# Which gaps the writes and sums of weight parts stand in: attention and gated MLP on one core

## The chip, the core and the metric

The kernel runs on one core of one Trainium2 chip. TensorE (PE) multiplies, VectorE (DVE) and ScalarE (ACT) work element by element, SyncE (SP) issues most of the DMAs (transfers between the chip's memory, called DRAM here, and the on-chip buffers). The metric is the device time of one launch in microseconds (us), the median of three runs.

## The reference

Two parts follow each other. In a chunked attention, each chunk of 32 queries sees 8 memory tokens, 16 tokens to the left, its own 32 and 8 to the right. Then the 3072 resulting tokens of width 512 go through an RMS norm and a gated MLP with 1536 features:

```python
for c in range(nc):                       # 4 batches x 8 heads, 24 chunks
    scores = scale * np.matmul(q_c, k_full.transpose(0, 1, 3, 2))
    scores = scores - np.max(scores, axis=-1, keepdims=True)
    a = np.exp(scores)
    a = a / (np.sum(a, axis=-1, keepdims=True) + 1e-09)
    out[:, :, c_start:c_end] = np.matmul(a, v_full)
...
x = np.ascontiguousarray(attn_out.transpose(0, 2, 1, 3)).reshape(B * S, H * D)
...
rms = np.sqrt(np.mean(x * x, axis=-1, keepdims=True) + 1e-06)
xn = x / rms * rms_g
g = xn @ w_gate
silu = g * (1.0 / (1.0 + np.exp(-g)))
val = xn @ w_val
return (silu * val @ w_out).astype(np.float32)
```

Every product of the MLP keeps float32 accuracy by splitting both factors into a high and a low part and adding three products: high by high, low by high, high by low.

## The kernel before

**Stages.** The tokens are cut in blocks of 384. An order written out by hand (`ORDER`) does the attention of the first two blocks, splits the first weights and starts the MLP. Then three segments follow: the rest of block 0 (features 5 to 11), block 2 (features 0 to 11) and block 3 (all twelve, 10 and 11 first). At the end `whole(2)` and `whole(3)` each take two blocks together, by a scheme with seven products in place of eight. It multiplies by sums and differences of weight quarters. These, and the plain weight parts, are read back from scratch in DRAM (the tiles `kept`: `kg` for the gate weight, `kv` for the value weight, `ko` for the output weight), which the segments write.

**A segment.** For the n-th feature group of 128 it issues 12 matmuls of the gate product (`pg`, L469), then calls `visit(2n)`, 12 of the value product (`pv`), `visit(2n+1)`, 9 of the output product of the feature before (`po`, L519), `visit(2n+1.5)`, and then the elementwise part of its own feature: a tanh (L483), the gate (L487, reading the bank `pg`), the product with `pv` (L490), its high part `hh` (L178) and low part `hl` (L499). The number that `visit` is called with is the gap. At the end of block 0 and block 2 the last feature takes another path: the gate product is copied to `rg` (L478), and after L487 and L490 the next block's x is split (L750) and the last `hh` is made (L753).

**What a gap does**, in this order:
- `dumps(k)` writes plain weight parts from their buffers to scratch: six DMAs on SyncE (L767), two of 256 KB, two of 128 KB and two of 256 KB. There are twelve such items. They are pinned behind the last DMA issued on SyncE so far.
- `keep(n)` spends a budget of n elements a partition on the weight sums, from the table `KEEP`. An item of sums has two additions 512 wide (high plus low part, L803, at 512 each of the budget), four additions or subtractions 256 wide (L806), four casts on ScalarE into the buffer `kh` (L810), two subtractions 512 wide (L815), and two writes of 512 KB on SyncE (L817 from `kh`, L819 from the sums `ks` or `qp1`). It costs 3072 of budget. There is a single `kh`, and it shares a buffer with `rg`: the casts of the next item wait until the write from it has ended.
- The letters in the table `VISITS` step the attention of a later pair of heads: "p" transposes the probabilities of the pair before (L279) and copies them out of their banks (L178 on ScalarE, L181 on VectorE); "s" makes the scores of the next pair (L216), takes maxima (L227), subtracts (L239), takes exponentials (L244), and, when these scores have been made, loads the queries (L163) and keys (L165) of the pair after into the same buffers; "o" (half a gap later) makes the value product of the pair (banks `oe` and `oo`, L310), evacuates it (L321, into `xT`), squares it (L324), and loads the next values (L170); "n" does a piece of the RMS norm.

**What sets the order.** TensorE's instructions stay in program order. The other engines' pieces are placed by a scheduler, within what `issue_after` pins, and each engine runs its queue in order: an instruction that waits holds all behind it. A DMA on SyncE that waits for its buffer does the same. Before the change, gaps 0 to 11 of block 0 call `dumps` once each.

Of the kernel before, what the change touches and what calls it, by code (L numbers as in the profile page):

```python
# [8 lines left out]
F32 = mybir.dt.float32  # L9
# [14 lines left out]
DM, FF = 512, 1536  # L24
P = 128
# [21 lines left out]
PAIRS = tuple((f, f + 1) for f in range(0, FF // P, 2))  # L47
NR = 30

KEEP = {0: {2: 1024, 3: 1024},  # L50
# [3 lines left out]

CHAIN = (("g", 1, "a", 1), ("g", 2, "c", 1), ("v", 1, "a", 1), ("g", 6, "a", 0), ("v", 2, "c", 1), ("g", 7, "a", 0),
         ("v", 6, "a", 0), ("g", 5, "e", 1), ("g", 4, "a", 0), ("v", 7, "a", 0), ("g", 3, "e", 0), ("v", 5, "e", 1),
# [30 lines left out]
def tile_kernel(ctx: ExitStack, tc: tile.TileContext, q, k, v, w_gate, w_val, w_out, rms_g, out):  # L87
# [11 lines left out]
    dram = ctx.enter_context(tc.tile_pool(name="dram", bufs=1, space=bass.MemoryType.DRAM))  # L99
# [174 lines left out]
    def stage_p(u, tag=None):  # L274
        d = st[u]
        t = psum_m(tag, f"pT{u}") if tag else psum_a(f"pT{u}")
        pe = d["p"].rearrange("p j k -> p (j k)")
        for i in range(NT):
            on_pe(nc.tensor.transpose(out=t[:, i * P:(i + 1) * P], in_=pe[:, i * P:(i + 1) * P], identity=ident))  # L279
        d["t"] = t  # L280
# [183 lines left out]
    def moe_in(n, f, xs, kts=range(NKT), ps=None):  # L464
        if ps is None:
            ps = psum_m(n, f"p{n}")
        for kt in kts:
            for i, (a, c) in enumerate(PASS):
                on_pe(nc.tensor.matmul(ps[:, 0:HT], lhsT=weight(a, n, f, kt), rhs=xs[c][:, kt],  # L469
                                 start=kt == 0 and i == 0, stop=kt == NKT - 1 and i == 2))  # L470
        return ps[:, 0:HT]
# [37 lines left out]
    def moe_h(g, vv, blk):  # L509
        t = moe_t(g, vv, blk)  # L510
        return moe_hl(t, moe_hh(t))

    def psm_o(i):
        return psum_m(f"o{i}", f"po{i}")

    def moe_out(f, h, po, first=0, end=NF - 1):
        for i in range(NT):
            for n, (a, c) in enumerate(PASS):
                on_pe(nc.tensor.matmul(po[i], lhsT=h[a][:, i * P:(i + 1) * P], rhs=weight(c, "o", f),  # L519
                                 start=f == first and n == 0, stop=f == end and n == 2))  # L520
# [4 lines left out]
    def store(blk, po):  # L525
        for i in range(NT):
            o = obuf(f"ob{i}")
            nc.scalar.activation(o, po[i], AF.Copy, scale=0.5 if blk > 1 else sh[blk][:, i:i + 1])
            nc.scalar.dma_start(out=out[blk * HT + i * P:blk * HT + (i + 1) * P], in_=o)
# [23 lines left out]
    def last_of(eng):  # L553
        return next(i for i in reversed(nc.cur_bb.bb.instructions) if i.engine == eng.engine)
# [136 lines left out]
    def tok_o(n):  # L691
# [10 lines left out]
        P=lambda n: stage_p(n, "o0" if n < NG else None),  # L702
# [58 lines left out]
    kept = {}  # L761

    def dump(f, w, cols, to):
        k, i, n = fgroup[f]
        for part in range(2):
            c = wt[part, w, k].bitcast(F32)[:, i * DM:(i + 1) * DM]
            nc.sync.dma_start(out=to[:, :, part], in_=c[:, cols].rearrange("p (k f) -> p k f", k=to.shape[1]))  # L767

    items, sums = [(p, w) for p in (5, 0, 1, 2, 3, 4) for w in "gv"], {}

    def dumps(k):
        p, w = items[k]
        fa, fb = PAIRS[p]
        kept[w, p] = t = dram.tile([P, 7, 2, DM // 2], F32, name=f"k{w}{p}")
        with tc.issue_after(last_of(nc.sync)):
            dump(fa, w, slice(0, DM), t[:, 0:2])
            dump(fb, w, slice(DM // 2, DM), t[:, 2:3])
            f = fa if w == "g" else fb
            kept["o", f] = t = dram.tile([P, 2, DM], F32, name=f"ko{f}")
            dump(f, "o", slice(0, DM), t.unsqueeze(1))  # L780

    def keep_steps():

        late_part = iter(())
        for k in range(len(items) + 1):
            now = keep_item(k) if k < len(items) else iter(())
            for _ in range(2):
                if k < len(items):
                    yield next(now)
            yield from late_part  # L790
            if k < len(items):
                for _ in range(4):
                    yield next(now)
            late_part = now

    def keep_item(k):
        p, w = items[k]
        fa, fb = PAIRS[p]
        s = (late["tmp"] if k % 2 else p1.tile([P, 2 * DM], F32, name="ks", tag="wy")).rearrange("p (k f) -> p k f", k=4)
        for i, f in enumerate((fb, fa)):  # L800
            c, n, _ = fgroup[f]
            h, l = (wt[part, w, c][:, n * DM:(n + 1) * DM].bitcast(F32).rearrange("p (k f) -> p k f", k=2) for part in range(2))
            nc.vector.tensor_tensor(out=s[:, 2 * i:2 * i + 2], in0=h, in1=l, op=ALU.add)  # L803
            yield DM
        for o, a, b, op in ((1, 0, 1, ALU.add), (0, 2, 0, ALU.subtract), (2, 1, 2, ALU.subtract), (3, 3, 2, ALU.subtract)):
            nc.vector.tensor_tensor(out=s[:, o], in0=s[:, a], in1=s[:, b], op=op)  # L806
            if o == 3:
                h = p1.tile([P, 3 * HT], F32R, name="kh", tag="rg")[:, 0:2 * DM].rearrange("p (k f) -> p k f", k=4)
                for i in range(4):
                    nc.scalar.copy(h[:, i], s[:, i])  # L810
            yield DM // 2
        l, t = s.bitcast(F32R), kept[w, p]
        for i in range(2):
            c = slice(2 * i, 2 * i + 2)
            nc.vector.tensor_tensor(out=l[:, c], in0=s[:, c], in1=h[:, c].bitcast(F32), op=ALU.subtract)  # L815
            if i:
                nc.sync.dma_start(out=t[:, 3:7, 0], in_=h.bitcast(F32))  # L817
                with tc.issue_after(last_of(nc.sync)):
                    nc.sync.dma_start(out=t[:, 3:7, 1], in_=s)  # L819
            yield DM  # L820

    keeping = keep_steps()

    def keep(n):
        with tc.issue_after(last_of(nc.vector)), tc.issue_after(last_of(nc.scalar)):
            while n > 0:
                n -= next(keeping, DM)
# [150 lines left out]
    for blk, fs in segments:  # L978
        po = [psm_o(i) for i in range(NT)] if blk else sp["po", 0]
        edge = dict(first=fs[0] if blk else 0, end=fs[-1])  # L980

        def visit(gap):
            if blk == 0 and gap in range(12):
                dumps((gap + 2) % 12)
            keep(KEEP[blk].get(gap, 0))
            for c in VISITS[blk].get(gap, ""):
                if next(todo) != c:
                    raise AssertionError(gap)
        for n, f in enumerate(fs):
            g = moe_in("g", f, xs)  # L990
            visit(2 * n)
            out_ = lambda f=fs[n - 1], h=prev: moe_out(f, h, po, **edge)
            if n == 0:
                out_ = lambda: None
                if blk == 0:

                    moe_out(NF - 1, prev, po1)
                    with tc.high_priority():
                        store(1, po1)
            vv = moe_in("v", f, xs)  # L1000
            visit(2 * n + 1)
            if n < len(fs) - 1:
                out_()
                visit(2 * n + 1.5)
                prev = moe_h(g, vv, blk)
                if blk == 3 and n == 2:
                    late_cm[1].__exit__(None, None, None)
                if blk == 3 and n == 7:
                    w0_cm.__exit__(None, None, None)
                    xpool = ctx.enter_context(tc.tile_pool(name="xs", bufs=1, reuse_waits="tile"))  # L1010
                    sup["ring"] = ctx.enter_context(tc.tile_pool(name="ring", bufs=NR, reuse_waits="tile"))
                    for m in (1, 2, 3, 6):
                        sup["xpool", m] = xpool
                    load(NR)
                    x_first(4)
                if blk == 3 and n == 9:
                    x_second(4)
            elif blk < 3:
                with tc.high_priority():
                    t = moe_t(g, vv, blk)  # L1020
                xs = split_x(late_x["x"], t, out_, lambda h: moe_out(fs[-1], h, po, **edge))
            else:
                with tc.high_priority():
                    h = moe_h(g, vv, blk)
                out_()
        if blk == 0:
            behind.close()
        if blk < 3:
            store(blk, po)
# [84 lines left out]
```

## Time and profile before

| what | value |
|---|---|
| time, median of 3 runs | 698.16 us (697.62 to 699.15) |
| the profiled execution | 696.32 us |
| its span, first to last instruction | 694.5 us |
| TensorE busy / VectorE / ScalarE | 667.8 / 471.5 / 305.0 us |
| moved by DMA | 140.19 MB, 202 GB/s over the span |

The profile is of one execution. Busy time of an engine is what its instructions take; a busy share near 100% says that the engine sets the pace there. In rows of the timeline the first number is the start in us from the span's start, the second the duration, then engine, line, operation, result and operands; brackets at the end give idle time of that engine just before it and what ended that. In rows of the view by windows stand the window, its length, busy time and instructions of PE, PEld (weight loads of TensorE), DVE, ACT and POOL, then the clock that TensorE was granted (1.00 is full speed), the share of time in which the DMA engines were busy, and GB/s. Rows of DMAs give the count, KB each, and the median us from issue to landing.

### The profile page before, as it was taken

Reading aid. Unit: us, or ns where it says so; the run is one execution under the profiler, and the core shown is the slowest. Engines: PE = TensorE matmul, PEld = TensorE weight load, DVE = VectorE, ACT = ScalarE, POOL = GpSimd, SP = SyncE. Lnnn points to the kernel's source line nnn. Section 1 sums busy time; section 2 is a strip of 40 time slices with the busy share of each in tenths; the row PEclk is TensorE's granted clock in tenths of the full one; section 3 lists DMA queues with packets and bytes.
Section 4 is the critical chain, followed back from the end, with each engine's and each line's share of the span. In section 5 each row is a group of like instructions: output and inputs, shape, how many; then the busy total and the mean of one; then the engine's idle time right before and its main releaser. Section 6 shows DMA issues by size and latency. Waiting matters only on the chain.

```text
span 694.5 us, 15083 instructions
## 1 busy us (share of the span) xinstructions
PE 667.8 (96%) x6134; PEld 609.5 (88%) x6134; DVE 471.5 (68%) x937; ACT 305.0 (44%) x566; POOL 4.7 (1%) x12
## 2 busy tenths in 40 slices
PE   7799999999699999999999999999999999999997
PEld 6698899998598898889999899998988899999885
DVE  6788999867478898867858766569639254555221
ACT  4787987832235444344234444343334343332112
POOL 0010000000000000000000000000000000000000
PEclk9999999999999999999999999999999999999999
DMA  9653643449996746337139688887643598885002
GB/s 326 248 179 126 238 156 106 148 153 371 322 375 233 232 152 203 116 99 254 58 108 356 234 255 282 266 294 237 192 143 123 177 301 252 251 254 160 0 1 91
DMA packets 79701, 140.19 MB, mean 202 GB/s; under 512 B 7440, under 2 KB 33040, under 8 KB 79632
## 3 DMA queue, kind: packets, MB, share of 16 engines
q1 hardware_dynamic: 77760, 136.08, 58.6%
q10 hardware_dynamic: 1872, 3.15, 1.2%
q8 instruction: 48, 0.79, 0.5%
q14 instruction: 21, 0.17, 0.1%
HBM read 104.60 MB, written 34.60 MB: 200 GB/s over the span
## 4 chain that ended last, share of the span: by engine, by line
PE 75%; DVE 11%; DMA 5%; ACT 5%; issue 2%; SPq 1%; ACTq 0%; DVEq 0%
PE po L957 14%; PE pv L469 10%; PE pg L469 10%; PE po L519 10%; PE mga L928 7%; PE mva L928 7%; PE mve L928 3%; PE mge L928 3%; PE oe L310 2%; PE mvc L928 2%; PE s L216 2%; PE pT L279 2%; DMA r<-kg 1%; PE mgc L928 1%; DVE t L487 1%
## 5 line engine op out<-in xcount | busy, mean ns | idle before, releaser
L957 PE MATMUL po<-r,hhs 128*128 128x512 f32 x288 | 90.7, 396 | 0.0
L469 PE MATMUL pv<-xh,wh_v 128*128 128x384 f32 x192 | 65.8, 343 | 2.2 <-DVE t L490 1.3
L469 PE MATMUL pg<-xh,wh_g 128*128 128x384 f32 x192 | 66.7, 347 | 0.4 <-DVE t L487 0.4
L469 PE MATMUL pg<-xl,wh_g 128*128 128x384 f32 x192 | 65.4, 341 | 0.5 <-DVE xl L654 0.5
L469 PE MATMUL pv<-xh,wl_v 128*128 128x384 f32 x192 | 65.1, 339 | 0.5 <-DVE wl_v L440 0.5
L469 PE MATMUL pg<-xh,wl_g 128*128 128x384 f32 x192 | 65.5, 341 | 0.0
L469 PE MATMUL pv<-xl,wh_v 128*128 128x384 f32 x192 | 65.1, 339 | 0.0
L957 PEld LDWEIGHTS po<-r,hhs 128*128 128x128 f32 x288 | 53.9, 188 | 12.4
L519 PE MATMUL po<-wh_o,hh 128*128 128x512 f32 x144 | 58.3, 405 | 0.8 <-ACT hh L753 0.4
L928 PE MATMUL mga<-x,r 128*128 128x384 f32 x288 | 58.3, 337 | 0.2 <-ACT spare L900 0.2
L928 PE MATMUL mva<-x,r 128*128 128x384 f32 x288 | 58.1, 337 | 0.1
L519 PE MATMUL po<-wh_o,hl 128*128 128x512 f32 x144 | 57.4, 398 | 0.0
L519 PE MATMUL po<-wl_o,hh 128*128 128x512 f32 x144 | 57.2, 397 | 0.0
L957 PE MATMUL po<-r,hls 128*128 128x512 f32 x144 | 56.8, 395 | 0.0
L939 DVE TENSOR_TENSOR hls<-h,hhs 128x768 fp32r<-128x768 f32 x24 | 22.9, 955 | 42.1 <-ACT hhs L938 42.1
L928 PEld LDWEIGHTS mga<-x,r 128*128 128x128 f32 x288 | 50.5, 188 | 1.0 <-ACT spare L900 0.5
L928 PEld LDWEIGHTS mva<-x,r 128*128 128x128 f32 x288 | 50.5, 188 | 0.5 <-DVE h L911 0.4
L178 ACT CAST hh<-t 128x384 fp32r<-128x384 f32 x46 | 23.7, 514 | 47.4 <-PE po L519 35.7
L938 ACT CAST hhs<-h 128x768 fp32r<-128x768 f32 x24 | 20.0, 835 | 54.4 <-PE po L957 50.5
L469 PEld LDWEIGHTS pv<-xh,wh_v 128*128 128x128 f32 x192 | 36.3, 189 | 4.0 <-DVE t L490 1.6
L469 PEld LDWEIGHTS pg<-xh,wh_g 128*128 128x128 f32 x192 | 36.3, 189 | 2.8 <-DVE t L487 0.9
L469 PEld LDWEIGHTS pg<-xl,wh_g 128*128 128x128 f32 x192 | 36.4, 189 | 2.1 <-DVE xl L654 0.7
(162 smaller groups left out, 1424.6 us busy)
## 6 DMA issues: line engine op xcount, KB each, us to landing
r<-kg SPq DMA_DIRECT2D x84, 256.0 KB, 3.3
r<-kv SPq DMA_DIRECT2D x84, 256.0 KB, 3.3
r<-ko SPq DMA_DIRECT2D x48, 256.0 KB, 3.1
kv<-in_v_dram SPq DMA_DIRECT2D x24, 384.0 KB, 5.3
kv<-in_k_dram SPq DMA_DIRECT2D x24, 312.0 KB, 4.7
ws<-in_moe_w_gate_dram SPq DMA_DIRECT2D x4, 1024.0 KB, 4.9
ws<-in_moe_w_val_dram SPq DMA_DIRECT2D x4, 1024.0 KB, 4.9
ws<-in_moe_w_out_dram SPq DMA_DIRECT2D x4, 1024.0 KB, 5.0
```

Of the source, the lines that this page charges most:

```text
L178: return nc.scalar.copy(out, in_)
L216: on_pe(nc.tensor.matmul(d["s"][a:a + CH, o:o + KC], lhsT=d["q"][r, c * CH:c * CH + CH], rhs=d["k"][r, c // 2, 40 * cp:40 * cp + KC], star ...
L279: on_pe(nc.tensor.transpose(out=t[:, i * P:(i + 1) * P], in_=pe[:, i * P:(i + 1) * P], identity=ident))
L310: on_pe(nc.tensor.matmul(o2[cp][64 * hh:64 * hh + 64, o:o + CH], lhsT=st[u]["v"][r, j, hh], rhs=pt[r, j, hh ^ u % 2], start=True, stop=True))
L469: on_pe(nc.tensor.matmul(ps[:, 0:HT], lhsT=weight(a, n, f, kt), rhs=xs[c][:, kt], start=kt == 0 and i == 0, stop=kt == NKT - 1 and i == 2))
L487: nc.vector.scalar_tensor_tensor(out=t, in0=t, scalar=1.0, in1=g, op0=ALU.add, op1=ALU.mult)
L519: on_pe(nc.tensor.matmul(po[i], lhsT=h[a][:, i * P:(i + 1) * P], rhs=weight(c, "o", f), start=f == first and n == 0, stop=f == end and n = ...
L928: on_pe(nc.tensor.matmul(bank[w, b], lhsT=r[:, a, kt], rhs=x[:, c, kt], start=bool(first) and kt == 0 and i == 0, stop=kt == 1 and i == 2, ...
L938: nc.scalar.copy(hh, sup["h", f])
L939: nc.vector.tensor_tensor(out=hl, in0=sup["h", f], in1=hh.bitcast(F32), op=ALU.subtract)
L957: on_pe(nc.tensor.matmul(po[i], lhsT=cur[a][:, i * P:(i + 1) * P], rhs=r[c], start=f == n == 0, stop=f == NF - 1 and n == 2))
```

## The change

Two tables change. `DUMPS` is new and says how many of the twelve items each gap writes, in the order in which they come: in block 0 one in gaps 1 and 2, none in gaps 3 to 7, then two, one, two, one, one and one in gaps 8 to 13, and the last two in gaps 0 and 1 of block 2. `KEEP` gets a gap 12 in block 0 (1536), gives up half of gaps 4 and 16 and all of gap 18 in block 2, and moves budget in block 3 from gap 4 to gaps 2 and 10. The scratch tiles are allocated up front. A line of the changed kernel has a number higher by 2 in most of the code, by 5 from the sums on.

```diff
-KEEP = {0: {2: 1024, 3: 1024},
-        2: {0: 512, 1: 2048, 2: 2048, 3: 2048, 4: 2048, 6: 512, 7: 1024,
-            8: 2048, 9: 2048, 10: 2048, 11: 2048, 12: 2048, 13: 2048, 14: 2048, 15: 2048, 16: 2048, 18: 512},
-        3: {2: 1024, 3: 2048, 4: 2048, 6: 512, 10: 1024}}
+KEEP = {0: {2: 1024, 3: 1024, 12: 1536},
+        2: {0: 512, 1: 2048, 2: 2048, 3: 2048, 4: 1024, 6: 512, 7: 1024, 8: 2048, 9: 2048, 10: 2048, 11: 2048, 12: 2048, 13: 2048,
+            14: 2048, 15: 2048, 16: 1024},
+        3: {2: 1536, 3: 2048, 4: 1024, 6: 512, 10: 3072}}
+
+DUMPS = {0: {1: 1, 2: 1, 8: 2, 9: 1, 10: 2, 11: 1, 12: 1, 13: 1}, 2: {0: 1, 1: 1}, 3: {}}
...
-    items, sums = [(p, w) for p in (5, 0, 1, 2, 3, 4) for w in "gv"], {}
+    items = [(p, w) for p in (5, 0, 1, 2, 3, 4) for w in "gv"]
+    for p, w in items:
+        kept[w, p] = dram.tile([P, 7, 2, DM // 2], F32, name=f"k{w}{p}")
 
     def dumps(k):
+        k = (k + 2) % len(items)
         p, w = items[k]
         fa, fb = PAIRS[p]
-        kept[w, p] = t = dram.tile([P, 7, 2, DM // 2], F32, name=f"k{w}{p}")
+        t = kept[w, p]
...
-    keeping = keep_steps()
+    keeping, dumping = keep_steps(), iter(range(len(items)))
...
         def visit(gap):
-            if blk == 0 and gap in range(12):
-                dumps((gap + 2) % 12)
+            for _ in range(DUMPS[blk].get(gap, 0)):
+                dumps(next(dumping))
             keep(KEEP[blk].get(gap, 0))
```

TensorE's list of instructions is the same before and after. On the other engines the order moves at these places.

**SyncE in block 0.** The queue of before at the loads of the visits at gap 5 (first four rows) and gap 7 (the rows behind the marks); `q0` and `qp1` are queries, `kv0` and `kv1` keys and values; of the 24 dump DMAs between them the first and the last three stand here:

```order
L163 DMA q0_1702<-in_q_dram 128x384
L165 DMA kv0_1704<-in_k_dram 128x624
L163 DMA qp1_1726<-in_q_dram 128x384
L165 DMA kv1_1727<-in_k_dram 128x624
L767 DMA kg1_1889<-wh_g1_90 128x2x256
...
L767 DMA kv2_1982<-wl_v3_1079 128x256
L767 DMA ko5_1987<-wh_o3_1080 128x512
L767 DMA ko5_1987<-wl_o3_1081 128x512
L163 DMA q0_1702<-in_q_dram 128x384
L165 DMA kv0_1704<-in_k_dram 128x624
L163 DMA qp1_1726<-in_q_dram 128x384
L165 DMA kv1_1727<-in_k_dram 128x624
```

And in the changed kernel, from the same loads on; between the two rows of dumps stand 52 more, nine items in all, and behind them come the first item's write from `kh` (L822) and from `ks`, then the last item's six:

```order
L165 DMA q0_1702<-in_q_dram 128x384
L167 DMA kv0_1704<-in_k_dram 128x624
L165 DMA qp1_1726<-in_q_dram 128x384
L167 DMA kv1_1727<-in_k_dram 128x624
L172 DMA kv0_1704<-in_v_dram 128x768
L172 DMA kv1_1727<-in_v_dram 128x768
L769 DMA kg1_1735<-wh_g1_90 128x2x256
...
L769 DMA ko10_2586<-wl_o6_1483 128x512
L822 DMA kg5_1731<-kh_1919 128x4x256
L824 DMA kg5_1731<-ks_1899 128x4x256
L769 DMA kv5_1732<-wh_v6_1480 128x2x256
```

The dumps have moved from between the loads to behind the last loads of block 0; the write from `kh`, which stood behind twelve items before too, is now nearer to block 2, since nine items are issued only after gap 7.

**VectorE at the end of block 0**, before (`hl` of the feature before, the copy of the last gate product, the gate, the value, then the split of x):

```order
L499 TENSOR_TENSOR hl_2503<-t_2497,hh_2501 128x384
L478 TENSOR_TENSOR rg_154<-pg_2505,rg_154 128x384
L487 SCALAR_TENSOR_TENSOR t_2532<-t_2532,rg_154 128x384
L490 TENSOR_TENSOR t_2532<-t_2532,pv_2518 128x384
L750 TENSOR_TENSOR xl_2537<-xT_1990,xh_2536 128x384
L754 TENSOR_TENSOR hl_2550<-t_2532,hh_2549 128x384
```

And after:

```order
L501 TENSOR_TENSOR hl_2475<-t_2469,hh_2473 128x384
L808 TENSOR_TENSOR qp1_1726<-wh_v7_1486,wl_v7_1487 128x512
L808 TENSOR_TENSOR qp1_1726<-wh_v6_1480,wl_v6_1481 128x512
L480 TENSOR_TENSOR rg_154<-pg_2477,rg_154 128x384
L489 SCALAR_TENSOR_TENSOR t_2521<-t_2521,rg_154 128x384
L492 TENSOR_TENSOR t_2521<-t_2521,pv_2500 128x384
L752 TENSOR_TENSOR xl_2526<-xT_1968,xh_2525 128x384
L820 TENSOR_TENSOR ks_1899<-ks_1899,kh_1919 128x512
L756 TENSOR_TENSOR hl_2539<-t_2521,hh_2538 128x384
```

Two additions of plain parts (gap 12's budget) stand ahead of the copy of the gate product, and one subtraction ahead of the last `hl`; before, all three came behind the split of x.

**VectorE at the first visit of block 2 (gap 5)**, before, from the copy of the transposed probabilities on:

```order
L181 COPY kv0_1704<-pT13_2727 128x384
L806 TENSOR_TENSOR qp1_1726<-qp1_1726 128x256
L227 TENSOR_REDUCE mx14_2783<-s14_2733 128x6
L227 TENSOR_REDUCE mx15_2787<-s15_2734 128x6
L239 TENSOR_TENSOR pe14_2785<-s14_2733,mx14_2783 128x384
L239 TENSOR_TENSOR pe15_2789<-s15_2734,mx15_2787 128x384
```

And after:

```order
L183 COPY kv0_1704<-pT13_2734 128x384
L820 TENSOR_TENSOR qp1_1726<-qp1_1726,kh_2616 128x512
L229 TENSOR_REDUCE mx14_2790<-s14_2740 128x6
L229 TENSOR_REDUCE mx15_2794<-s15_2741 128x6
L820 TENSOR_TENSOR qp1_1726<-qp1_1726,kh_2616 128x512
L808 TENSOR_TENSOR ks_2621<-wh_g1_90,wl_g1_91 128x512
L808 TENSOR_TENSOR ks_2621<-wh_g0_84,wl_g0_85 128x512
L241 TENSOR_TENSOR pe14_2792<-s14_2740,mx14_2790 128x384
L241 TENSOR_TENSOR pe15_2796<-s15_2741,mx15_2794 128x384
```

The item of sums in work here is an earlier one than before. Behind these rows, ahead of the next gate (L487 before, L489 after), stand two more L806 and two L803 before; four L811 and two L820 after.

**ScalarE at the same place**, after: the copy of the transposed probabilities, the four casts into `kh`, and what queues behind them.

```order
L180 COPY pt0_1703<-pT12_2730 128x384
L815 CAST kh_2616<-qp1_1726 128x256 x4
L180 CAST hh_2888<-t_2884 128x384
L246 ACTIVATE pe14_2792<-pe14_2792 128x384
L246 ACTIVATE pe15_2796<-pe15_2796 128x384
L323 COPY xT_2729<-oe12_2813 128x12x32
```

Before, four casts stood ahead of the copy, and two pairs of casts into the next `kh` behind the first exponential.

At the second visit of block 2 (gap 17), two L803, two L815 and three L806 stand between L181 and the end of L239 after the change; before, three L806 and two L803. At the first visit of block 3 (gap 1), two L815 and one L803 stand ahead of the maxima, where one L815 and two L806 stood. At gap 10 of block 3, with its budget of 3072, two L806 and one L815 stand between `hl` and the gate.

## The prediction

> **What bounds the kernel now.** I read the page first: the shares of the engines, then the chain that ended last.
>
> ```profile
> span 694.5 us, 15083 instructions
> PE 667.8 (96%) x6134; PEld 609.5 (88%) x6134; DVE 471.5 (68%) x937; ACT 305.0 (44%) x566; POOL 4.7 (1%) x12
> PE 75%; DVE 11%; DMA 5%; ACT 5%; issue 2%; SPq 1%; ACTq 0%; DVEq 0%
> ```
>
> TensorE is busy 96% of the span and three quarters of the chain. The change leaves its list of instructions as it was, so it can only give or take time in which TensorE stands still. The next view is therefore that of TensorE's waits, in the stretch from 75 to 400 us that holds blocks 0, 2 and 3, where every edit lies (the first row; the figures are us in total, times, and the longest one).
>
> ```profile
> PE s L216 <- DMA kv<-in_k_dram: 5.3, 2, 3.8
> ```
>
> One stop stands out: 5.3 us of scores matmuls waiting for a key load. The timeline, TensorE alone, shows what it costs in full. The first three rows are the undisturbed visit at gap 5 of block 0 (transposes, the last scores, the value product), the others the visit at gap 7.
>
> ```profile
> 169.95 0.82 PE L279 MATMUL pT<-ident,pe 128*128 128x128 f32 x6
> ...
> 171.63 0.23 PE L216 MATMUL s<-kv,qp 64*32 64x64 f32 x2
> ...
> 174.10 0.25 PE L310 MATMUL oe<-pt,kv 64*64 64x32 f32 x2
> ...
> 180.24 0.27 PE L279 MATMUL pT<-ident,pe 128*128 128x128 f32 x1
> 184.86 0.30 PE L216 MATMUL s<-kv,q 64*32 64x64 f32 x4 [3.79 <-DMA kv<-in_k_dram]
> ...
> 191.18 0.25 PE L310 MATMUL oe<-pt,kv 64*64 64x32 f32 x2
> ```
>
> From transposes to value product it is 4.15 us at gap 5 and 10.94 at gap 7: the stop costs **6.79 us**, more than its two waits. The rest is the clock, in the view by windows:
>
> ```profile
> 186.30:189.80 3.50, 3.12 (x96) 2.69 (x97) 1.54 (x4) 0.02 (x1) 0.00 (x0) 0.51 1.06 390
> 186.20:212.00 25.80, 25.32 (x298) 23.11 (x298) 18.56 (x43) 8.33 (x19) 0.00 (x0) 0.93 1.05 373
> ```
>
> After the idle time the granted clock is 0.51 for 3.5 us (third figure from the end of the first row). Why the load is late stands in SyncE's queue:
>
> ```profile
> 180.65 0.43 SPq L165 DMA_DIRECT2D kv<-in_k_dram  x1
> ...
> 193.87 0.85 SPq L170 DMA_DIRECT2D kv<-in_v_dram  x2
> ...
> kv<-in_v_dram SPq DMA_DIRECT2D x5, 384.0 KB, 6.2
> kv<-in_k_dram SPq DMA_DIRECT2D x6, 312.0 KB, 5.0
> ```
>
> The buffers were free when the scores of gap 5 ended, at 171.63 + 0.23, but 24 dump DMAs stood ahead, so the last key load went out at 180.65 and needed some 5 us to land (last figure of the DMA view's rows).
>
> **Part 1, loads ahead of dumps: minus 6.8 us.** In the new order SyncE has nothing between the loads for gap 5 and those for gap 7. They go out at about 172 and, at 5.0 us to landing, are there by 178.5; the scores are due when the transposes are through, 0.82 after 180.24. More than two microseconds of room, so the whole 6.79 goes. What is late next is the transposed probabilities' copy, which the 4.15 us of gap 5 already contain.
>
> **Part 2, two additions in front of the last gate of block 0: plus 1.2 us.** Rows of VectorE, ScalarE and TensorE there, and the time of the additions (two of 512 in 1.28 us, 0.60 each since the second's end overlaps the next piece; two of 256 in 0.88):
>
> ```profile
> 208.70 0.55 DVE L499 TENSOR_TENSOR hl<-t,hh 128x384 fp32r<-128x384 f32 x1
> 209.16 0.55 DVE L478 TENSOR_TENSOR rg<-pg,rg 128x384 f32<-128x384 f32 x1
> 214.61 1.28 DVE L803 TENSOR_TENSOR qp<-wh_v,wl_v 128x512 f32<-128x512 f32 x2
> ...
> 217.02 0.88 DVE L806 TENSOR_TENSOR qp<-qp 128x256 f32<-128x256 f32 x2
> ...
> 210.96 1.33 ACT L810 CAST kh<-ks 128x256 fp32r<-128x256 f32 x4
> 212.19 0.51 ACT L753 CAST hh<-t 128x384 fp32r<-128x384 f32 x1
> ...
> 212.75 0.50 PE L519 MATMUL po<-wh_o,hh 128*128 128x512 f32 x1 [0.39 <-ACT hh L753]
> ```
>
> L478 follows L499 without idle time, and from it a chain (tanh, gate, four casts, hh) ends in a wait of TensorE of 0.39 us already. Two L803 between L499 and L478 move all of it by 2 x 0.60 = 1.2. Nothing hides them.
>
> **Part 3, the dump backlog at the first visit of block 2 (gap 5): about plus 0.2.** From here on the changed kernel is 6.8 - 1.2 = 5.6 us ahead of the times of before. The dumps start when the value loads of gap 7 are out, at 193.87 - 6.8 = 187.1. An item is 2 x 256 + 2 x 128 + 2 x 256 KB = 1.31 MB. Ahead of the first item's write from kh stand 9 items (11.8 MB), two value loads (0.8), three stores of block 0's result (256 KB each, 0.8) and that write itself (0.5): 13.9 MB. At the 373 GB/s of the window above (last figure) this takes 37.3 us, to about 224.4. ScalarE's next use of kh, four casts, stands right behind this row, which ends at 230.89 - 5.6 = 225.3:
>
> ```profile
> 230.41 0.48 ACT L178 COPY pt<-pT 128x384 f32<-128x384 f32 x1 [1.74 <-PE pT L279]
> 231.09 0.55 DVE L181 COPY kv<-pT 128x384 f32<-128x384 f32 x1
> 239.59 0.55 DVE L487 SCALAR_TENSOR_TENSOR t<-t,pg 128x384 f32<-128x384 f32 x1
> 235.74 0.24 PE L310 MATMUL oo<-pt,kv 64*64 64x32 f32 x1 [0.70 <-issue]
> 242.98 0.34 PE L469 MATMUL pg<-xh,wh_g 128*128 128x384 f32 x1
> ```
>
> So kh is free in time, by 0.9 us. But VectorE now has eight pieces of plain sums between L181 and L487, where it had five: two L815, two L803, four L806 and two L815 more against three L806 and two L803, some 2.5 us more at 0.45 to 0.60 each, and its last two wait for casts that wait for the next kh write, behind another item. That puts L487 at about 236.8, and the next gate product, which reuses the bank that L487 reads, is due at 236.5 without the 0.70 us of "issue". It starts at 237.3 in place of 237.2 with the old stop: about even, and 0.2 is taken. Bounds: minus 0.7 (the stop of "issue" goes, the chain keeps up) to plus 3 (kh frees 3 us late); the value lies nearest to the row of 373 GB/s.
>
> The Trainium skill, "DMA: Bandwidth & Descriptors", section "Specifications", gives a core about 358 GB/s of HBM. By that the backlog would take an estimated 38.8 us and free kh 0.6 us late, and the gain would be about 2.6 us in place of 3.2. The row says 373, and goes.
>
> **Part 4, second visit of block 2 (gap 17): plus 0.9.** Now, on VectorE, ScalarE and TensorE:
>
> ```profile
> 273.77 0.55 DVE L181 COPY kv<-pT 128x384 f32<-128x384 f32 x1
> 277.88 1.29 DVE L803 TENSOR_TENSOR ks<-wh_g,wl_g 128x512 f32<-128x512 f32 x2 [1.38 <-DMA kg<-ks]
> 279.09 1.02 DVE L239 TENSOR_TENSOR pe<-s,mx 128x384 f32<-128x384 f32 x2
> 280.93 0.48 ACT L321 COPY xT<-oo 128x384 f32<-128x384 f32 x1
> 281.47 0.44 PE L469 MATMUL pv<-xh,wh_v 128*128 128x384 f32 x1 [0.85 <-ACT xT L321]
> ```
>
> From the start of L181 to the end of L239 pass 6.34 us, 1.38 of them a wait. In the new order two L803, two L815 and three L806 stand between them, with no wait if the scratch writes keep pace: 7 pieces and 6 of attention and MLP make 6.5 us. Two of ScalarE's casts (0.7 us) also come between the exponentials and the evacuation. The stop of 0.85 grows by 0.2 + 0.7. Bounds: minus 0.85 to plus 2.
>
> **Part 5, first visit of block 3: plus 0.5.** Two L815 and an L803 stand ahead of the maxima where an L815 and two L806 stood (2.25 us for 1.4 with the L806 that is left), and one cast fewer (0.4) ahead of the evacuation.
>
> ```profile
> 310.58 0.24 PE L310 MATMUL oe<-kv,kv 64*64 64x32 f32 x1 [1.38 <-issue]
> 312.57 0.48 ACT L321 COPY xT<-oo 128x384 f32<-128x384 f32 x1
> 313.10 0.44 PE L469 MATMUL pv<-xh,wh_v 128*128 128x384 f32 x1
> ```
>
> The value product starts 0.05 us after the evacuation's end, so it would have been held even without the "issue" stop. It comes 0.5 us later. Bounds: minus 0.5 to plus 1.4.
>
> **Part 6, gap 10 of block 3: plus 0.7.** Two L806 and an L815 stand ahead of this gate, for whose bank the transposes wait:
>
> ```profile
> 343.49 0.55 DVE L499 TENSOR_TENSOR hl<-t,hh 128x384 fp32r<-128x384 f32 x1
> 344.66 0.55 DVE L487 SCALAR_TENSOR_TENSOR t<-t,pg 128x384 f32<-128x384 f32 x1 [0.62 <-ACT t L483]
> 345.27 0.33 PE L279 MATMUL pT<-ident,pe 128*128 128x128 f32 x1 [0.20 <-DVE t L487]
> ```
>
> They need 2 x 0.45 + 0.60 = 1.5 us from 343.95, so L487 starts at 345.4 in place of 344.66. Bounds 0 to 0.9. The remaining moves, in gaps 7 to 15 of block 2, I cost at nothing: the budgets of these gaps are the same as before, and the gate product gives VectorE room before its bank is wanted again (L487 ends at 239.59 + 0.55, the bank is written at 242.98, 2.84 later). Without that cover a gap's pair of additions costs 1.2.
>
> **Sum.** -6.8 + 1.2 + 0.2 + 0.9 + 0.5 + 0.7 = -3.3, taken as -3.2 since the terms are rounded. The profiled execution took 696.32 us (span 694.5), which gives 693.1; it was 1.84 under the median of the runs, 698.16, so the median after should be **695.0**.
>
> **Rivals.** (a) The pieces are absorbed and only the load's stop goes, perhaps with the 0.85 of gap 17: 698.16 - 6.8 = 691.4, or 690.5. For it speaks that VectorE is busy 68% only; against it that L478, L239 and L487 are each the last to arrive in the rows above. Chance 0.20. (b) The backlog moves the stop from gap 7 of block 0 to gap 5 of block 2. The place is ScalarE's four casts into kh, behind which hh, the exponentials and the evacuation queue; every microsecond that kh frees after 225.3 is one of TensorE's. A slower pace stands in the window over the first dumps and the loads of gap 7:
>
> ```profile
> 150.00:186.00 36.00, 31.27 (x434) 28.02 (x432) 21.19 (x54) 10.61 (x21) 0.00 (x0) 1.00 1.00 333
> ```
>
> At 333 GB/s the 13.9 MB take 41.7 us, to 228.8, 3.5 us late. That stands in place of the 0.2 and eats the gain (-3.5 + 3.5 = 0); if a stop of this length brings the half clock too, as the 3.79 at gap 7 did, it costs the same again as there, 6.79 - 5.3 = 1.5: 699.7. It decides from a landing at about 228 on. For it speaks that SyncE's queue holds all nine items without a gap; against it that the rate behind the stop was 373 and 390. Chance 0.22, of which two thirds end near no change (697.5) and one third slower. (c) The load of gap 7 is late all the same, and only parts 2 to 6 remain: 698.16 + 3.5 = 701.7. Only if it took 9 us to land; the longest row above has 6.2. Chance 0.03. The forecast itself (minus 1.4 to minus 5) has 0.52, and 0.03 is for what I have not seen.
>
> **Numbers.** 0.2% (1.4 us) is about what a measurement of this kernel can tell from no change. Faster: 0.52 + 0.20 less 0.01, 0.71; slower: 0.07 of (b), 0.03 of (c), 0.02 unseen, 0.12; same: the rest, 0.17. The range reaches from (a), 691.0, to the near half of (b), 698.8, and leaves out 2 in 10.
>
> **What would show it.** Right: no wait of L216 for a key load in block 0, granted clock 1.00 there; the wait of L519 for hh at block 0's end at 1.6 us; pv for xT at gap 17 near 1.7; transposes of gap 11 in block 3 waiting 0.9. ScalarE's four casts in block 2 showing a wait for the kh write of over 1 us would speak for (b). Wrong outright: a scores matmul that still waits in block 0, or parts 2 to 6 of which two or more show no wait.

## The result, and the profile after

| | before | after |
|---|---|---|
| median | 697.89 us, 4 runs (695.75 to 699.15) | 706.93 us, 4 runs (706.01 to 708.0) |
| ratio to before | | 1.0133, 95% interval 1.0104 to 1.0163 |
| profiled execution / its span | 696.32 / 694.5 us | 706.01 / 704.2 us |

The kernel became 1.3% slower; 695.0 had been predicted, with a range up to 698.8. The page of the changed kernel: span, busy time of the engines, and the shares of the chain that ended last.

```profile
span 704.2 us, 15081 instructions
PE 670.7 (95%) x6134; PEld 611.7 (87%) x6134; DVE 470.9 (67%) x937; ACT 303.5 (43%) x566; POOL 4.7 (1%) x12
PE 73%; DVE 12%; ACT 6%; SPq 4%; DMA 3%; issue 2%; ACTq 0%; DVEq 0%; POOL 0%; POOLq 0%
```

The work is the same; TensorE only stands still more. SyncE's queue (SPq) now has 4% of the chain, where it had 1%. TensorE's waits between 75 and 420 us (us in total, times, longest):

```profile
PE pg L471 <- DVE t L489: 9.3, 3, 7.5
PE pv L471 <- ACT xT L323: 2.7, 2, 1.7
PE po L521 <- ACT hh L755: 1.7, 1, 1.7
PE ssum L340 <- ACT sh L335: 1.1, 1, 1.1
PE oe L312 <- issue: 1.1, 1, 1.1
PE pv L471 <- DVE t L492: 0.8, 1, 0.8
PE pT L281 <- DVE t L489: 0.8, 1, 0.8
```

The wait of the scores for a key load, 5.3 us before, is not in the list. In its place stands one of 7.5 us for the gate. TensorE at gap 7 of block 0, its first transposes and the first value product:

```profile
180.39 0.81 PE L281 MATMUL pT<-ident,pe 128*128 128x128 f32 x6
184.54 0.25 PE L312 MATMUL oe<-pt,kv 64*64 64x32 f32 x2
```

That is 4.15 us, as at the undisturbed gap 5; the change did what it says. The time went away some 25 us later. ScalarE at the end of block 0 (ACTq are DMAs that it issues), then SyncE's queue, then TensorE:

```profile
208.43 0.69 ACT L530 ACTIVATE ob<-po,srh 128x512 f32<-128x512 f32 x1
216.28 0.34 ACTq L531 DMA_DIRECT2D out_dram<-ob  x1
216.72 1.27 ACT L530 ACTIVATE ob<-po,srh 128x512 f32<-128x512 f32 x2 [7.60 <-DMA ko<-wh_o]
218.46 1.86 ACTq L531 DMA_DIRECT2D out_dram<-ob  x2
220.37 0.49 ACT L485 ACTIVATE t<-pg 128x384 f32<-128x384 f32 x1 [2.38 <-DMA kv<-wl_v]
...
213.64 0.45 SPq L769 DMA_DIRECT2D ko<-wh_o  x1
216.66 0.68 SPq L769 DMA_DIRECT2D kv<-wl_v  x1
...
221.50 0.69 PE L471 MATMUL pg<-xh,wh_g 128*128 128x384 f32 x1 [7.48 <-DVE t L489]
```

ScalarE evacuates the first third of block 0's result at 208.43 and then stands for 7.6 us. What it waits to do is not the next evacuation but the DMA between them: the first store goes out at 216.28, 2.64 us behind the issue of a dump on SyncE, `ko<-wh_o`, to which the profile puts the wait down. The third store waits in the same way for `kv<-wl_v`. Behind the stores stands the tanh of block 2's first feature (L485), behind that the gate (L489), and TensorE wants the gate's bank back. The order in which the changed kernel issues, with the semaphores that each DMA waits for (`_49` is part of their names), says why a store depends on a dump that reads other data. SyncE's row stands first, then ScalarE's, eight DMAs behind it in the order that the scheduler expected:

```
L769 DMA ko8_2494<-wh_o4_1086 128x512 [waits DMAHW6_49]
L531 DMA out_0_dram<-ob0_2557 128x512 [waits DMAHW6_49,Activation_49]
```

The program hands eight DMA semaphores (DMAHW0 to 7) in turn to all DMAs of SyncE and ScalarE, in the order that the scheduler expected, and a DMA may only be issued when the one that had its semaphore before it has landed. The scheduler had placed the first store behind `ko9`; SyncE was still at `kv3`, fourteen DMAs earlier, when the store was ready at 209.1. Two further places, VectorE first, then the wait of TensorE that follows, at gap 17 of block 2 and behind gap 1 of block 3:

```profile
287.91 0.69 DVE L808 TENSOR_TENSOR ks<-wh_g,wl_g 128x512 f32<-128x512 f32 x1 [2.35 <-DMA kg<-ks]
290.33 0.44 PE L340 MATMUL ssum<-sh,one 128*128 128x384 f32 x1 [1.13 <-ACT sh L335]
...
323.21 0.69 DVE L808 TENSOR_TENSOR qp<-wh_v,wl_v 128x512 f32<-128x512 f32 x1 [2.50 <-DMA kv<-qp]
326.49 0.44 PE L471 MATMUL pg<-xh,wh_g 128*128 128x384 f32 x1 [1.70 <-DVE t L489]
```

In both, an addition of weight parts waits until the write from its buffer has landed, and VectorE's work for TensorE queues behind it. Last, the view by windows of the changed kernel (last three figures: granted clock, DMA share, GB/s):

```profile
150.00:176.00 26.00, 26.00 (x404) 23.47 (x402) 17.48 (x45) 7.78 (x15) 0.00 (x0) 1.00 0.69 232
176.00:187.00 11.00, 11.00 (x244) 9.94 (x237) 6.75 (x15) 5.10 (x11) 0.00 (x0) 1.00 0.61 194
187.00:228.00 41.00, 31.85 (x153) 29.35 (x152) 24.32 (x54) 11.40 (x25) 0.00 (x0) 0.88 1.02 348
221.40:227.20 5.80, 5.70 (x18) 5.70 (x19) 1.71 (x4) 1.00 (x2) 0.00 (x0) 0.50 1.02 353
```

and of the kernel before:

```profile
150.00:176.00 26.00, 25.91 (x401) 23.06 (x399) 17.19 (x46) 7.86 (x16) 0.00 (x0) 1.00 1.03 355
```

Before, the DMA engines were full from 150 us on. The new table leaves them idle for 31% of 26 us and 39% of 11 us, 12.4 us in all or three items at 1.31 MB and 348 GB/s, and that work stands in the queue behind gap 7. The clock behind the stop is 0.50 for 5.8 us.

Matching TensorE's groups of matmuls in both traces, the profiled execution lost and gained: gap 7 of block 0 minus 6.8; end of block 0 plus 1.3; start of block 2 plus 7.6, and its half clock plus 2.7; the old stop of issue at gap 5 of block 2 minus 1.0; gap 17 plus 0.9 and 1.2; gap 1 of block 3 plus 1.0, and plus 1.9 behind it; gap 11 plus 0.6; the rest, small steps either way, near zero. Together plus 9.4, of the 9.7 by which the span grew.

### The profile page after: what moved, and what is told of

The parts are those of the page before. It is cut to its first block, busy times and chain, and to the rows that moved or that the text cites. A ratio compares the mean times of both kernels' runs of the same rounds, so it can differ in the third digit from the quotient of the medians.

```text
span 704.2 us, 15081 instructions
## 1 busy us (share of the span) xinstructions
PE 670.7 (95%) x6134; PEld 611.7 (87%) x6134; DVE 470.9 (67%) x937; ACT 303.5 (43%) x566; POOL 4.7 (1%) x12
## 4 chain that ended last, share of the span: by engine, by line
PE 73%; DVE 12%; ACT 6%; SPq 4%; DMA 3%; issue 2%; ACTq 0%; DVEq 0%; POOL 0%; POOLq 0%
PE po L962 14%; PE pg L471 10%; PE po L521 9%; PE pv L471 9%; PE mga L933 6%; PE mva L933 6%; PE mge L933 3%; PE mve L933 3%; SPq L769 3%; PE mvc L933 2%; PE pT L281 2%; PE s L218 2%; PE mgc L933 1%; PE oe L312 1%; DMA kg<-wh_g 1%
## 5 line engine op out<-in xcount | busy, mean ns | idle before, releaser
L471 PE MATMUL pg<-xh,wh_g 128*128 128x384 f32 x192 | 68.5, 357 | 9.4 <-DVE t L489 9.3
L962 PEld LDWEIGHTS po<-r,hhs 128*128 128x128 f32 x288 | 53.9, 188 | 12.4
```

Of the source, the lines that this page charges most:

```text
L962: on_pe(nc.tensor.matmul(po[i], lhsT=cur[a][:, i * P:(i + 1) * P], rhs=r[c], start=f == n == 0, stop=f == NF - 1 and n == 2))
```

## The experiments

**Theory S**: the store's issue on ScalarE, held by the semaphore of a dump, is what costs. **Theory K**: it is the backlog of dumps as such, and the store is only the first place where it shows. A third question was how much the new table of sums costs by itself. All timed runs, each beside the kernel before on the same chip (medians of 697.6 to 698.35 there); rows from different chips are best compared by their ratios:

| dumps | sums | stores | median us | ratio, 95% interval |
|---|---|---|---|---|
| new | new | ScalarE (the change, again) | 703.79 | 1.0113 (1.0078 to 1.0147) |
| new | new | GpSimd | 706.3 | 1.0109 (1.0061 to 1.0157) |
| new | new | GpSimd, again | 702.8 | 1.0071 (1.0036 to 1.0106) |
| new | old | ScalarE | 701.22 | 1.0043 (1.0020 to 1.0066) |
| new | old | GpSimd | 698.75 | 1.0003 (0.9982 to 1.0024) |
| old | new | ScalarE | 700.59 | 1.0046 (1.0020 to 1.0073) |
| new, two earlier | new | ScalarE | 698.54 | 1.0008 (0.9988 to 1.0028) |
| early | old | ScalarE | 694.43 | 0.9960 (0.9940 to 0.9980) |
| early | old | GpSimd | 692.88 | 0.9938 (0.9914 to 0.9962) |
| early, tail in block 2 | old | ScalarE | 691.73 | 0.9894 (0.9870 to 0.9919) |
| early, tail in block 2 | new | ScalarE | 695.0 | 0.9949 (0.9919 to 0.9979) |
| new, tail in block 2 | new | ScalarE | 691.98 | 0.9918 (0.9874 to 0.9963) |

### The stores of block 0 from another queue

```diff
-            nc.scalar.dma_start(out=out[blk * HT + i * P:blk * HT + (i + 1) * P], in_=o)
+            (nc.scalar if blk else nc.gpsimd).dma_start(out=out[blk * HT + i * P:blk * HT + (i + 1) * P], in_=o)
```

> The changed kernel, with one edit: the three stores of block 0's result are issued from GpSimd's queue in place of ScalarE's. Theory S (ScalarE is held at block 0's first store, because that DMA may only be issued when a dump eight DMAs ahead of it has landed): ScalarE's idle time of 7.6 us ahead of the second evacuation is gone, TensorE's wait of 7.5 us for the gate at the start of block 2 too, and with it the half clock behind it (some 2.7 us): 706.9 - 10.2 = 696.7, or up to 3 us more if the casts into kh are now the next to wait for the dumps. Rival K (the dumps as such slow block 2, by bandwidth or through kh, whoever issues the store): 703 or more, with TensorE's stop near 221 us in another place but as long.

The profiled execution took 701.33 us, and the stop was gone: the second gate product of block 2 is not in its list of waits up to 230 us. But three other runs took 705 to 707.6, and the median is 706.3, where theory S had at most 699.7. ScalarE in the profile, and TensorE behind it:

```profile
227.26 1.02 ACT L815 CAST kh<-qp 128x256 fp32r<-128x256 f32 x3 [1.93 <-DMA kg<-kh]
237.39 1.32 ACT L815 CAST kh<-ks 128x256 fp32r<-128x256 f32 x4 [3.07 <-DMA kv<-kh]
...
239.95 0.44 PE L471 MATMUL pg<-xh,wh_g 128*128 128x384 f32 x1 [2.07 <-DVE t L489]
```

The casts into `kh` now wait for the writes from it, which stand in SyncE's queue behind the dumps: the mechanism of rival (b), with the store out of its way. Since median and profile lay 5 us apart, it was run again, beside the changed kernel.

> The changed kernel as it is, as the reference for the runs beside it and to see how steady its stops are. 706 to 708; ScalarE's wait ahead of block 0's second evacuation 7 to 8 us, TensorE's stop behind it 7 to 8.

> The changed kernel with block 0's stores on GpSimd's queue once more, since its profiled execution (701.3) and the median of its four runs (706.3) were 5 us apart. If the store's issue is what costs (theory S), the median is some 5 under that of the changed kernel beside it (701 to 703), and what remains are waits of ScalarE's casts into kh for a scratch write, at gap 5 of block 2 and behind it. If the dumps cost as much whoever issues the store (theory K), it is within 2 of the changed kernel.

The changed kernel took 703.79 (702.71 to 706.98), less than the 706 to 708 expected, the one with released stores 702.8 (698.13 to 706.54). By the medians they are 1 us apart, by the ratios 0.4%, some 3 us, and the intervals overlap: the 10.2 of theory S is out, a few us are not. The changed kernel's own second profile (702.71) has the stop of the gate product again, 6.92 us. But there the norm's sums do not wait at all, and the wait behind gap 1 of block 3 is 0.40 in place of 1.70: these two differ between executions of one kernel. In the second profile with released stores (705.16) no store held ScalarE, but one cast into `kh` waited 5.27 us and an addition 3.71:

```profile
237.82 1.32 ACT L815 CAST kh<-ks 128x256 fp32r<-128x256 f32 x4 [5.27 <-DMA kv<-kh]
...
284.69 0.69 DVE L808 TENSOR_TENSOR ks<-wh_g,wl_g 128x512 f32<-128x512 f32 x1 [3.71 <-DMA kg<-ks]
```

So S names the right place and the wrong price. The store is where the backlog is paid first; when it is released, half of it or all is paid at the next waits. Matched group by group as above, the first profile with released stores had gained 10.4 us on that of the changed kernel at 218 us and had given 5.7 of them back by the end; the second had gained 8.5 on the profile beside it at 216 us and lost 10.2 behind. What issuing from GpSimd costs by itself was not measured apart. The Trainium skill, "DMA: Bandwidth & Descriptors", section "Issuing engines are not separate DMA queues", has a rule for this: transfers of all issuing engines run on the same DMA engines, and another queue saves only the issuing time. The runs agree: 7.6 us of ScalarE's time were freed, and the median moved by about 1.

### One table at a time

> Only the new table of dumps, with the table of sums of before. Theory S: the key load's stop is gone (-6.8), the store's stop and its half clock are there (+10.2 less 1.0 for the stop of issue at gap 5), the stops at the ends of block 0 and in gap 17 and block 3 are those of before: 697.9 + 2.4 = 700.3. If the table of sums is what made the stop: 691 to 692.

> Only the new table of sums, with the dumps of before (one in each of gaps 0 to 11 of block 0). Theory S: no stop at the store, the key load's wait of 5.3 us as before, and the stops that the changed kernel shows at block 0's end (+1.3), gap 17 of block 2 (+0.9 and +1.2 at the norm's sums), gap 1 to 2 of block 3 (+1.0 and +1.9) and gap 11 of block 3 (+0.6), some 0.8 given back: 697.9 + 6 = 704. If those stops come only from the late dumps: 698 to 699.

> The new dumps, the old sums, block 0's stores on GpSimd's queue: what the released store is worth without the new sums. If the store's wait is the whole price of the backlog: 701.2 less 8.2 (6.5 of stop, 1.7 of half clock) = 693. If the waits for scratch writes take its place as they did with the new sums: 698 to 701, with ScalarE's casts into kh or VectorE's sums waiting several us for DMA between 225 and 260.

Only the dumps: 701.22 (700.3 expected), with the store's wait (6.8 us on ScalarE) and this stop:

```profile
220.92 0.69 PE L471 MATMUL pg<-xh,wh_g 128*128 128x384 f32 x1 [6.34 <-DVE t L489]
```

Only the sums: 700.59, where I had 704. The stops at block 0's end and in block 3 are there (some 2.5 us more than before at gap 1 and behind it), those of gap 17 are not, and even the old wait of 0.85 there is gone. The run with the dumps alone has both at gap 17, 0.94 and 2.02; in the changed kernel they come with the dumps. With the old sums and the store released: 698.75, 2.5 less than with the store held, where 8 would have gone if the store were all. ScalarE shows why:

```profile
232.13 1.33 ACT L815 CAST kh<-qp 128x256 fp32r<-128x256 f32 x4 [4.18 <-DMA kg<-kh]
239.21 1.33 ACT L815 CAST kh<-ks 128x256 fp32r<-128x256 f32 x4 [4.03 <-DMA kv<-kh]
```

### Two items earlier

```diff
-DUMPS = {0: {1: 1, 2: 1, 8: 2, 9: 1, 10: 2, 11: 1, 12: 1, 13: 1}, 2: {0: 1, 1: 1}, 3: {}}
+DUMPS = {0: {1: 1, 2: 1, 3: 1, 4: 1, 8: 1, 9: 1, 10: 1, 11: 1, 12: 1, 13: 1}, 2: {0: 1, 1: 1}, 3: {}}
```

> The changed kernel with two dump items moved from gaps 8 and 10 to gaps 3 and 4 of block 0, so two fewer behind gap 7. By bytes alone the dumps end 7.5 us earlier and the stop goes (-10.2: 696.7). By theory S it shrinks less, since in the new order of issue the third store takes the semaphore that a dump ten DMAs later than before has held (the second write of the gate weight's half of feature 7): in the changed kernel that one went out at 222.2, here some 7.6 earlier, and lands about 217.2; ScalarE's tanh then starts at about 217.4 in place of 220.4, TensorE's stop is 4 to 5 us in place of 7.5, and the time 703 with a little less half clock.

ScalarE and TensorE:

```profile
213.95 0.35 ACTq L531 DMA_DIRECT2D out_dram<-ob  x1
214.40 1.27 ACT L530 ACTIVATE ob<-po,srh 128x512 f32<-128x512 f32 x2 [4.75 <-DMA ko<-wl_o]
216.69 0.49 ACT L485 ACTIVATE t<-pg 128x384 f32<-128x384 f32 x1 [1.03 <-DMA kg<-wl_g]
...
217.82 0.69 PE L471 MATMUL pg<-xh,wh_g 128*128 128x384 f32 x1 [3.31 <-DVE t L489]
```

The tanh started at 216.69 (217.4 expected), TensorE stopped for 3.3 us, not for 0 as the bytes alone would have it: how long the store waits follows from which dump had its semaphore. The time, 698.54, was better than the 703 expected: the wait of the norm's sums and the one of 1.7 us behind gap 1 of block 3 are not in its list either. But the second profile of the changed kernel lacks the one and nearly all of the other too, so this does not show that the two items took them away.

### Dumps early, and the tail elsewhere

Only the tables of dumps are shown; which table of sums goes with each stands in the table above.

```diff
 # early
+DUMPS = {0: {0: 1, 1: 1, 2: 1, 3: 1, 6: 1, 7: 1, 8: 1, 9: 1, 10: 1, 11: 1, 12: 1, 13: 1}, 2: {}, 3: {}}
 # early, tail in block 2
+DUMPS = {0: {0: 1, 1: 1, 2: 1, 3: 1, 6: 1, 7: 1, 8: 1, 9: 1, 10: 1}, 2: {18: 1, 19: 1, 20: 1}, 3: {}}
 # new, tail in block 2
+DUMPS = {0: {1: 1, 2: 1, 8: 2, 9: 1, 10: 2, 11: 1}, 2: {18: 1, 19: 1, 20: 1, 21: 1}, 3: {}}
```

> The sums of before, and dumps in gaps 0 to 3 and 6 to 13 of block 0, one each: two more stand ahead of the loads for gap 7, in time in which the changed kernel's SyncE waits, and all twelve are issued by the time of block 0's stores. Theory S: no key load stop (-6.8), the store waits at most 1.5 us, nothing else new: 691 to 692.5. If the dumps behind gap 7 cost time wherever they end (rival K): 695 or more.

> The sums of before, dumps in gaps 0 to 3 and 6 to 13 (as in the earlier run, 694.4), and block 0's stores on GpSimd's queue. Theory S: the stop of 2.5 us that this run still had at the start of block 2, with 2.3 of half clock behind it, goes: 694.4 - 4.8 = 689.6, up to 691. Theory K: 694 again.

Early dumps took 694.43, between the two expectations. The key load's stop was gone, the store's was not: the first store left at 215.06, and the gate product stopped for 2.50 us.

```profile
215.06 0.35 ACTq L531 DMA_DIRECT2D out_dram<-ob  x1
215.51 1.26 ACT L530 ACTIVATE ob<-po,srh 128x512 f32<-128x512 f32 x2 [4.46 <-DMA ko<-wl_o]
...
218.41 0.44 PE L471 MATMUL pg<-xh,wh_g 128*128 128x384 f32 x1 [2.50 <-DVE t L489]
```

With the store released 692.88, again between the two: 1.6 less and not 4.8; a cast into `kh` then waited 4.5 us. So the tail of the dumps was taken out of the way of both.

> The sums of before; dumps in gaps 0 to 3 and 6 to 10 of block 0, one each, and the last three in gaps 18 to 20 of block 2, where no sums are written. If the cost lies in the dumps still queued on SyncE when block 0's stores and the first writes of sums are due (the backlog theory, which both the store's wait and the kh waits belong to), nothing is queued there now: no key load stop, no stop at the start of block 2, casts into kh wait no more than before: 697.8 - 6.8 = 691, at most 1 off. If writes late in block 2 collide with the loads and sums of block 3: 694 or more.

> The same dumps with the new table of sums: the price of that table without a backlog. The run with the new sums and the old dumps was 2.4 above the kernel before, so 691 + 2.4 = 693.4; TensorE's wait for the last hh of block 0 1.7 us as there. If the table costs what the changed kernel shows from gap 17 on (some 6): 697.

> The changed kernel with one edit: its last four dump items move from gaps 12 and 13 of block 0 and 0 and 1 of block 2 to gaps 18 to 21 of block 2; the quiet gaps 3 to 7 and the double items in gaps 8 and 10 stay. Six items are left behind gap 7: 187 + 6 x 3.8 = 210, about when the first store is due. Backlog theory: the store waits at most 1 to 2 us, the casts into kh little, and the time is that of the run with late gaps and new sums, 693 to 695. If ten items bunched behind gap 7 are not what costs: 700 or more.

With the tail in block 2, where that block's sums end, and the old sums: 691.73, as expected, and the lowest median of all. With the new sums 695.0 (693.4 expected), 3.3 more (the sums alone had cost 2.2 on the old dumps). The third kernel is the change with nothing else altered than where its last four items go: 691.98 (693 to 695 expected), by the ratios some 2% under the change and 0.8% under the kernel before. ScalarE at block 0's end in that kernel:

```profile
206.56 0.69 ACT L530 ACTIVATE ob<-po,srh 128x512 f32<-128x512 f32 x1
207.53 0.36 ACTq L531 DMA_DIRECT2D out_dram<-ob  x1
208.31 1.27 ACT L530 ACTIVATE ob<-po,srh 128x512 f32<-128x512 f32 x2 [1.06 <-PE po L521]
```

The store goes out at once. That alone would fit theory S too. But releasing only the store had moved the ratio by 0.2 to 0.4%, on either table of sums, and taking four items out of the queue moves it by 2%, some 14 us (the intervals leave room down to 10). This speaks for theory K: ten items behind gap 7 cost, these six do not. The number is not all: the early dumps also leave six behind gap 7, with one each in gaps 6 and 7, and there SyncE reached the last of them at 215.6 us, here at 207.6. Between the new and the old sums these runs don't settle more than that the difference lies between 0 and some 3 us, since 691.98 and 695.0 both have the new ones and their runs spread (689.6 to 696.3, 692.1 to 696.1).

## Why the prediction was wrong

- All the signs that I had named for being right came: no wait for a key load in block 0, the clock at 1.00, and the waits of 1.67, 1.74 and 0.83 us. They tested parts 1, 2, 4 and 6. For part 3 there was only one, the casts into `kh`, and in the changed kernel these did not wait.
- **Part 1** was right: 10.94 us became 4.15, 6.79 gained, and the clock stayed at 1.00.
- **Part 2** was right: TensorE's wait for the last `hh` grew from 0.39 to 1.67 us, 1.28 for 1.2. The run with the new sums alone shows 1.60.
- **Part 3** failed, and with it the forecast: plus 0.2 was said, with bounds of minus 0.7 and plus 3, and it was 7.6 of stop and 2.7 of half clock less the 1.0 of issue, 9.3. The step that failed reads "three stores of block 0's result (256 KB each, 0.8)". They were counted as bytes ahead of the write from `kh`. They are also instructions in ScalarE's queue, ahead of everything that ScalarE does for block 2, and their issue waits for a dump. I asked when the dumps would free `kh` at 225 us, and not what else waits on a DMA between 187 and 225 us; the order that I looked at past the dumps was SyncE's alone. The waits are in the order of issue of the changed kernel, beside the very rows that the document shows. Two slips bear on nothing: the pieces of sums listed there are ten, not eight, and 242.98 - 5.6 is 237.4, not 237.2.
- The rate in part 3 was too high too: 348 GB/s between 187 and 228 us, against the 373 that I took. The write from `kh` was only issued at 224.19, when I had it landed. The Trainium skill, "DMA: Bandwidth & Descriptors", section "Specifications", gives about 358 GB/s of HBM for a core, which was nearer than my row.
- **Rival (b)** had the cause, the backlog, and put it at the wrong place and at too small a price (699.7). Its place showed as soon as the store was released: casts into `kh` that wait 1.93, 3.07 and 5.27 us.
- **Part 4**: the stop before the value product at gap 17 grew from 0.85 to 1.74, 0.89 for 0.9. But "with no wait if the scratch writes keep pace" did not hold: an addition waited 2.35 us, and the norm's sums 1.13. With the new sums on the old dumps this gap costs nothing, so my 0.9 had the right size for a wrong reason, by luck.
- **Part 5** was too small: 1.0 in place of 0.5 at gap 1, and 1.9 behind it, where an addition waits 2.50 us for its buffer's write. I had priced VectorE's pieces as work, not as pieces that wait for their own earlier write. The waits of 1.2 in gap 17 and 1.9 here stand in no term. With them the parts other than 3 come to about zero in this execution, in place of the -3.5 forecast for them; in the second profile of the changed kernel most of these two is absent.
- **Part 6** was right: 0.63 for 0.7.
- **Rival (c)** was rightly small. **Rival (a)** is about what comes out when the backlog is taken away: 691.7 and 692.0, for 691.4 or 690.5.

## What to carry to other kernels

When transfers are moved, count the DMA time that their old place filled and that the new one leaves idle: it comes back as a queue, here three items of 3.8 us, and it is paid at the first deadline behind it. Then look for every instruction that waits for any DMA while the queue lasts, on the other engines as well, with the semaphores in the compiled order and not the data alone: a store on an engine that also computes is such a deadline. Where releasing the first wait barely moves the time, move the backlog itself, into gaps in which nothing waits for a write.

## What the runs showed of the hardware

A DMA issued by ScalarE held that engine for 7.6 us, though its data was ready and it shares no data with the DMA that it waited for.

TensorE's clock fell after shorter stops than I had expected. The windows behind the stop of 2.50 us (early dumps) and its continuation:

```profile
218.40:222.00 3.60, 3.59 (x12) 3.59 (x13) 1.87 (x4) 0.52 (x2) 0.00 (x0) 0.55 1.02 354
222.00:224.00 2.00, 2.00 (x13) 2.00 (x12) 1.26 (x3) 1.70 (x5) 0.00 (x0) 0.95 0.48 163
```

The granted clock is 0.55 for 3.6 us, so this stop cost its length and 1.6 us again, in proportion more than the stop of 7.48 with its 2.7. The Trainium skill, "TensorE: Matmul & The Clock Gate", section "Part 1: The HAM clock gate (the "warmup" mystery)", puts the fall to half clock behind an idle window of about 3.4 us; here 2.50 us were enough, and the measurement decides. Nor is 2.50 a threshold. In the second run with released stores a stop of 2.24 us was enough as well (first row below); in the first run with them the stop of 2.07 shown above left the clock at full speed (second row):

```profile
325.60:329.00 3.40, 3.31 (x11) 3.31 (x12) 2.35 (x5) 0.51 (x1) 0.00 (x0) 0.52 0.00 0
239.90:243.90 4.00, 3.95 (x22) 3.95 (x23) 3.75 (x8) 1.19 (x4) 0.00 (x0) 1.00 0.80 286
```

Nor does the length of the stop set how long the half clock lasts: it was 5.8 us behind the stop of 7.48, and 3.2 us (at 0.52) behind the 6.92 of the changed kernel's second profile.

One thing stays open: the runs with the released stores spread from 698.1 to 707.6 us, and since one execution of each run was profiled, what the longer ones waited for was seen only in the two profiles, of 701.33 and 705.16.
